# An attention and two-MLP kernel whose order is planned from a table of costs: the costs and the priorities are replaced

## The chip, the core and the metric

The kernel runs on one core of a Trainium2 chip. The metric is the time of one execution on the device, in microseconds (us). TensorE (PE in the rows) does the matmuls, VectorE (DVE) and ScalarE (ACT) the elementwise work, GpSimd (POOL) next to nothing here, and the queues of SyncE (SP) and ACT issue the transfers.

## What is computed

Attention over 2 batches of 8 heads, 768 positions of 64 values, in which a query sees only the keys of its own hash bucket (6 sign bits of a projection); then two MLPs on the 1536 tokens, the first with a softplus, the second with a hard swish.

```python
mask = q_bucket[:, :, :, None] == k_bucket[:, :, None, :]
scores = np.where(mask, scale * np.matmul(q, k.transpose(0, 1, 3, 2)), -1000000000.0)
attn = np.exp(scores - np.max(scores, axis=-1, keepdims=True))
attn = attn / (np.sum(attn, axis=-1, keepdims=True) + 1e-09)
x = np.matmul(attn, v)                     # then heads side by side: 1536 x 512
h = x @ w_in                               # 512 x 2048, float64 weights
x = (np.maximum(h, 0.0) + np.log1p(np.exp(-np.abs(h)))) @ w_out
h = x @ w2_in
out = (h * np.clip(h + 3.0, 0.0, 6.0) / 6.0) @ w2_out
```

## The kernel before

**Attention.** There are 16 heads, and each has six tiles of 128 queries. `prepare` (L296) loads a head, splits q and k into a high part (`qa`, `ka`, on ACT at L331 and L243) and a low part (`qb`, `kb`, on DVE at L338 and L248), computes the hash products `d` on PE (L373) and turns them into bits that are sent to spare rows of `qb` and `kb`. `attend` (L419) does per tile t: four score matmuls into `sc` (L431, L432), the row maximum on DVE (`nm`, L445), a bias and scale (`bs`, L452), the exponential on ACT (`e`, L460), six transposes on PE into `tp` (L471), and a copy out of PSUM to `et` (L243 on ACT, or L245 on DVE for tiles 0 and 3). When a head's six tiles are done, the products with v go to `av` (L487) in three pieces of four; then come a copy `xa`, three transposes `pt` (L509), the normalisation `xn` (L524), and for every second head six transposes `xt` (L551) that lay the result out as MLP input.

`sc` and `tp` share three PSUM buffers (`THREE`), so a new `sc` can be written only when the `tp` that was three buffers ahead of it has been copied out. All of `raw`, `qa`, `ka`, `qb`, `kb` have two buffers, so head h+2 takes the place of head h: `ka` of head h+2 can be written only when head h's last score has been computed.

**MLPs.** `hidden` (L646) multiplies tokens with `w_in` into `ph` (L656), `activation` (L671) works on ACT and DVE, `project` (L737) multiplies with `w_out` into `acc` (L749, L751). A product is made of three matmuls, with high and low parts. The weights are float64 in memory; `convert` (L577) makes two float32 parts of each of the 64 blocks, with two operations on ACT and five on DVE. Sixteen blocks (`lows`) are loaded on ACT's queue and converted while attention runs, the other 48 in the MLPs. The first `hidden` matmul is planned after the last score of head 15 (`gate["hidden"]`).

**What sets the order.** No order is written by hand. Every piece of work is an operation with a cost per engine, and `Schedule.run` (L105) plays them through: it takes the engine and time that end first, and among the operations that could start there the one with the lowest `prio`. A head's priorities are `h * TH` plus a number from the table `WHEN`. The engines then execute exactly the order that came out, each its own, one after the other. So the costs and priorities leave no trace in the program but the order, and on which of two engines a copy stands. A `lows` block may not be converted before its `early` time (L580), nor loaded before `early - 12`.

Of the kernel before, what the change touches and what calls it, by code (L numbers as in the profile page):

```python
# [15 lines left out]
AF = mybir.ActivationFunctionType  # L16
# [19 lines left out]
TH = 10.540  # L36
WHEN = dict(load_p=-19.19, load_k=-22.30, load_q=-10.44, load_v=-16.15, high_k=-3.85, high_q=-7.91, low_k=7.98, low_q=-13.35, copy_q=2.17, dots=-7.44, bits=-3.01, send=-4.68, scores=0.99, max=-17.09, exp=5.00, turn=1.96, even=3.05, values=19.12, back=24.61, rec=19.19, norm=8.42, x=22.28, x_high=27.35, x_low=11.84)
# [10 lines left out]
STEP = 6.328  # L48
PROJECT = 9.472
ACTIVATE = -20.197  # L50
FETCH = -64.944
AHEAD = 22.618


def f32(ap):
    return ap.bitcast(F32)

# [22 lines left out]
class Schedule:  # L80
# [8 lines left out]
    def add(self, cost, emit, reads=(), writes=(), prio=0.0, after=(), uses=(), dma=0.0, mode="r", early=0.0):  # L89
# [15 lines left out]
    def run(self):  # L105
# [3 lines left out]
        while ready:  # L109
# [48 lines left out]
    def times(self, op):  # L158

        return {  # L160
            e: max([op.early] + [d.done + (SAME[e] if d.engine == e else CROSS) for d in op.deps]) for e in op.cost
        }

    def free(self, b, tag, taken):
# [7 lines left out]
        return max([o.done + CROSS for o in ring[i].users], default=0.0)  # L172
# [14 lines left out]
def lsh_attention_two_mlps(  # L187
# [90 lines left out]
    for s0, e in ((0, "S"), (D, "A")):  # L278
        plan.add(
            {e: 0.625 if e == "S" else 0.06}, lambda e, s0=s0: engines[e].dma_start(out=p32.ap[s0 : s0 + D, :], in_=proj),  # L280
            writes=[p32], prio=WHEN["load_p"], dma=0.06,
        )
# [13 lines left out]
    def prepare(h):  # L296
# [7 lines left out]
        queue = dict(S=0.625, A=0.06)  # L304
        first = queue if h > 1 else dict(S=0.625)
        plan.add(
            first, lambda e: engines[e].dma_start(out=raw.ap[0:D, :], in_=kv[head][0:D, :S]),
            writes=[raw], prio=at + WHEN["load_k"], dma=0.55,
# [3 lines left out]
            writes=[raw], prio=at + WHEN["load_k"], dma=0.55,  # L312
        )
        if h:
# [3 lines left out]
                writes=[rawk], prio=at + WHEN["load_q"], dma=1.1,  # L318
            )
        plan.add(  # L320
            dict(S=0.625),
            lambda e: engines[e].dma_start(out=vx[h].ap, in_=kv[head][:, S:].rearrange("p (c d) -> p c d", d=D)),
            writes=[vx[h]], prio=at + WHEN["load_v"], dma=1.1,
        )

        wide, narrow = dict(A=0.74) if h else dict(A=0.74, D=0.48), dict(D=0.88)
# [16 lines left out]
        if h:  # L343
            plan.add(
                wide, lambda e: cast(e, ka[h].ap, rawk.ap),
                reads=[rawk], writes=[ka[h]], prio=at + WHEN["high_k"],
            )
        else:
            for s0, e in ((0, "D"), (D, "A")):
                plan.add(  # L350
                    {e: wide[e]}, lambda e, s0=s0: cast(e, ka[h].ap[s0 : s0 + D, :], raw.ap[0:D, :]),
# [3 lines left out]
            narrow, lambda e: minus(e, kb[h].ap[0:D, :], raw.ap[0:D, :], f32(ka[h].ap[0:D, :])),  # L355
            reads=[raw, ka[h]], writes=[kb[h]], prio=at + WHEN["low_k"],
        )
        if h:
            plan.add(
                queue, lambda e: engines[e].dma_start(out=f32(qb[h].ap[0:D, :]), in_=f32(qa[h].ap[D:P, :])),  # L360
                reads=[qa[h]], writes=[qb[h]], prio=at + WHEN["copy_q"], dma=0.55,
            )
        else:
            plan.add(
                dict(A=0.74), lambda e: cast(e, qb[h].ap[0:D, :], f32(qa[h].ap[D:P, :])),
# [12 lines left out]
        plan.add(dict(T=0.68), dot, mode="c", reads=[raw, hashes], writes=[dots], prio=at + WHEN["dots"])  # L378
        if h == 0:
            for u in range(2):  # L380
                for n, x in enumerate((qb, kb)):
                    rows = slice((2 * u + n) * ROWS, (2 * u + n + 1) * ROWS)
                    plan.add(
                        dict(D=0.5),
# [15 lines left out]
        for u in range(2):  # L400
            for n, x in enumerate((qb, kb)):
# [6 lines left out]
                    reads=[bits], writes=[x[h]], prio=at + WHEN["send"], dma=0.15,  # L408
# [5 lines left out]
    def attend(h):  # L414
# [19 lines left out]
        for t in range(NT):  # L434
# [3 lines left out]
            for u in range(2):  # L438
                last_scores = plan.add(
                    dict(T=0.356), lambda e, sc=sc, t=t, u=u: scores(sc, t, u),  # L440
# [3 lines left out]
                dict(D=0.88),  # L444
# [6 lines left out]
                dict(D=0.1),  # L451
# [6 lines left out]
            exp = plan.add(  # L458
                dict(A=1.08),
# [13 lines left out]
            plan.add(dict(T=0.5), turn, mode="t", reads=[ex, ident], writes=[tp], prio=step + WHEN["turn"])  # L473

            def even(e, tp=tp, t=t):
# [4 lines left out]
                dict(A=0.73) if t % 3 else dict(A=0.73, D=0.88), even, reads=[tp], writes=[et[t // n]], prio=step + WHEN["even"],  # L480
# [12 lines left out]
        for c in range(0, NT, 2):  # L493
            last = [
                plan.add(
                    dict(T=1.36), mode="c", emit=lambda e, c=c: [some(c), some(c + 1)],
# [5 lines left out]
            dict(A=0.44), lambda e: cast(e, xa.ap, av.ap[:, :HALF]),  # L502
# [8 lines left out]
        plan.add(dict(T=0.25), back, mode="t", reads=[xa, ident], writes=[pt], prio=at + WHEN["back"])  # L511
# [17 lines left out]
        plan.add(dict(D=0.5), norm, reads=[pt, rec], writes=[x], prio=at + WHEN["norm"])  # L529
        return last_scores, exp  # L530
# [11 lines left out]
    def to_features(hp_all, first, n):  # L542
# [6 lines left out]
        def turn(e):  # L549
# [3 lines left out]
        plan.add(dict(T=0.085 * n), turn, mode="t", reads=[xn[hp_all], ident], writes=[pt], prio=at + WHEN["x"])  # L553
        hi = plan.add(
            dict(A=0.053 + 0.107 * n), lambda e: cast(e, place(xh), pt.ap[:, : n * P]),
# [3 lines left out]
            dict(D=0.069 + 0.133 * n), lambda e: minus(e, place(xl), pt.ap[:, : n * P], f32(place(xh))),  # L559
# [17 lines left out]
    def convert(layer, j, i, prio, after=()):  # L577

        before = layer == 0 and (j, i) in lows
        early = (lows.index((j, i)) + 1) * B * H * TH / (len(lows) + 1) if before else 0.0  # L580
# [18 lines left out]
        queue = dict(A=0.06) if before else dict(S=0.625)  # L599
# [204 lines left out]
    for h in range(B * H):  # L804
        prepare(h)
        last_scores, exp = attend(h)
        if h == 0:
            first_exp = exp
# [68 lines left out]
```

## Time and profile before

| | us |
|---|---|
| median of 3 runs | 804.89 |
| lowest and highest | 803.55, 804.92 |
| the profiled execution's own time | 804.03 |
| its span in the trace | 802.2 |
| PE, DVE, ACT busy in it | 776.2, 533.9, 483.8 |

The span runs from the first instruction to the last; the execution's time holds 1.8 us around it. An instruction's listed time is from its own start to its end, and instructions of one engine overlap a little, so the pace of an engine is read from start to start. In the trace a matmul of full float32 (`av`, `d`) stands as two instructions.

### The profile page before, as it was taken

The page shows a single profiled execution, that of the slowest core. Times are in us where ns is not written, and L with a number is a line of the kernel's source. Part 1 is how long each engine was busy: PE and PEld are TensorE (multiplying, and loading weights), DVE is VectorE, ACT ScalarE, POOL GpSimd, SP SyncE. Part 2 cuts the span into 40 slices and gives each one's busy share as a digit, 9 for nine tenths or more (in the row PEclk, how much of TensorE's full clock was granted, in tenths as well). Part 3 has the DMA queues.
Part 4 walks back from the last instruction along what each step waited for, and adds up shares of the span by engine and source line. Part 5 has one row for each costly group of instructions (what it writes and reads, how often), then busy time and mean ns, then how long its engine had stood idle before and what let it go on. Part 6 is the DMA issues. An engine that isn't in the chain of part 4 may idle for free.

```text
span 802.2 us, 10347 instructions
## 1 busy us (share of the span) xinstructions
PE 776.2 (97%) x3808; PEld 598.8 (75%) x3808; DVE 533.9 (67%) x942; ACT 483.8 (60%) x817; POOL 9.3 (1%) x53
## 2 busy tenths in 40 slices
PE   6799999999999999999999999999999999999997
PEld 3566666666667788888888888878888888888886
DVE  6699899886765899965554789999972322232222
ACT  4688998888875877766556677765642322231222
POOL 1000000000000000000000000000000000000000
PEclk9999999999999999999999999999999999999999
DMA  6545445432310460000000355640000100010001
GB/s 177 164 139 144 125 150 151 120 113 77 90 31 11 160 259 2 0 1 1 0 1 1 92 196 192 203 149 9 1 0 1 54 0 1 1 52 1 1 0 53
DMA packets 26355, 58.61 MB, mean 73 GB/s; under 512 B 3585, under 2 KB 7553, under 8 KB 26305
## 3 DMA queue, kind: packets, MB, share of 16 engines
q1 hardware_dynamic: 22128, 49.56, 20.2%
q10 hardware_dynamic: 4176, 8.39, 3.4%
q8 instruction: 30, 0.49, 0.3%
q14 instruction: 21, 0.16, 0.1%
HBM read 48.89 MB, written 3.15 MB: 65 GB/s over the span
## 4 chain that ended last, share of the span: by engine, by line
PE 87%; ACT 7%; DVE 3%; DMA 2%; issue 1%; SPq 0%; ACTq 0%; DVEq 0%
PE ph L656 33%; PE acc L749 17%; PE acc L751 16%; PE av L487 7%; PE tp L471 6%; PE sc L431 4%; PE sc L432 3%; ACT e L460 3%; ACT et L243 2%; DMA raw<-in_moe_w_in_dram 1%; ACT qa L331 1%; DVE nm L445 1%; ACT ka L243 1%; PE pt L509 1%; DVE qa L338 0%
## 5 line engine op out<-in xcount | busy, mean ns | idle before, releaser
L656 PE MATMUL ph<-xh,w 128*128 128x512 f32 x768 | 239.0, 393 | 0.0
L656 PEld LDWEIGHTS ph<-xh,w 128*128 128x128 f32 x768 | 144.0, 188 | 31.7
L656 PE MATMUL ph<-xl,w 128*128 128x512 f32 x384 | 150.4, 392 | 0.0
L685 DVE SCALAR_TENSOR_TENSOR ml<-me,ph 128x512 f32<-128x512 f32 x48 | 33.0, 688 | 114.1 <-ACT me L680 113.9
L460 ACT ACTIVATE e<-sc,bs 128x768 f32<-128x768 f32 x96 | 94.8, 989 | 22.5 <-DVE bs L452 21.9
L445 DVE TENSOR_REDUCE nm<-sc 128x1 f32<-128x768 f32 x96 | 89.5, 951 | 25.7 <-PE sc L432 25.4
L680 ACT ACTIVATE me<-ph,three 128x512 f32<-128x512 f32 x48 | 33.0, 688 | 122.0 <-PE ph L656 118.9
L749 PE MATMUL acc<-gh,w 128*128 128x512 f32 x384 | 98.3, 394 | 0.0
L751 PE MATMUL acc<-w,gh 128*128 128x512 f32 x384 | 97.4, 392 | 0.0
L471 PEld LDWEIGHTS tp<-ident,e 128*128 128x128 f32 x576 | 63.6, 142 | 37.1 <-ACT e L460 22.4
L471 PE MATMUL tp<-ident,e 128*128 128x128 f32 x576 | 80.0, 280 | 7.2 <-ACT e L460 6.2
L749 PEld LDWEIGHTS acc<-gh,w 128*128 128x128 f32 x384 | 71.7, 188 | 17.4 <-ACT gh L243 0.8
L751 PEld LDWEIGHTS acc<-w,gh 128*128 128x128 f32 x384 | 72.2, 188 | 16.2
L656 PEld LDWEIGHTS ph<-xl,w 128*128 128x128 f32 x384 | 72.2, 188 | 15.9
L431 PE MATMUL sc<-ka,qa 128*128 128x384 f32 x192 | 73.3, 382 | 6.1 <-ACT et L243 5.4
L487 PE MATMUL av<-et,vx 128*64 128x384 f32 x384 | 71.4, 498 | 0.0
L243 ACT ACTIVATE et<-tp 128x768 f32<-128x768 f32 x78 | 62.5, 811 | 12.6 <-PE tp L471 11.9
L432 PE MATMUL sc<-kb,qb 96*128 96x384 f32 x192 | 66.5, 346 | 0.4 <-DVE kb L385 0.4
L716 DVE SCALAR_TENSOR_TENSOR me<-mu,me 128x512 f32<-128x512 f32 x48 | 33.1, 690 | 38.3 <-ACT mu L711 38.1
L749 PE MATMUL acc<-gl,w 128*128 128x512 f32 x192 | 53.4, 393 | 0.7 <-ACT xh L243 0.7
L243 ACT ACTIVATE gh<-ml 128x512 fp32r<-128x512 f32 x48 | 30.1, 628 | 38.3 <-DVE ml L728 38.3
L751 PE MATMUL acc<-w,gl 128*128 128x512 f32 x192 | 53.1, 391 | 0.0
(65 smaller groups left out, 957.0 us busy)
## 6 DMA issues: line engine op xcount, KB each, us to landing
raw<-in_moe_w_out_dram SPq DMA_DIRECT2D x30, 512.0 KB, 4.2
raw<-in_moe_w_in_dram SPq DMA_DIRECT2D x18, 512.0 KB, 4.7
raw<-in_moe_w_in_dram ACTq DMA_DIRECT2D x14, 512.0 KB, 4.1
rawk<-in_kv_dram SPq DMA_DIRECT2D x15, 384.0 KB, 3.5
raw<-in_kv_dram SPq DMA_DIRECT2D x16, 192.0 KB, 3.6
raw<-in_q_dram SPq DMA_DIRECT2D x16, 192.0 KB, 3.7
vx<-in_kv_dram SPq DMA_DIRECT2D x16, 192.0 KB, 2.6
out_dram<-y SPq DMA_DIRECT2D x12, 256.0 KB, 2.0
```

Source lines behind the costliest of these rows:

```text
L243: nc.scalar.activation(out, in_, AF.Copy)
L431: nc.tensor.matmul(o, qa[h].ap[:, qs], ka[h].ap[:, cs], start=True, stop=False)
L432: nc.tensor.matmul(o, qb[h].ap[0:KB, qs], kb[h].ap[0:KB, cs], start=False, stop=True)
L445: lambda e, sc=sc, t=t: nc.vector.reduce_max(nm.ap[:, t, 0:1], sc.ap[:, :, :HALF], axis=AX.XY, negate=True),
L460: lambda e, sc=sc, ex=ex, t=t: nc.scalar.activation(ex.ap.rearrange("p (u k) -> p u k", u=2), sc.ap[:, :, :HALF], AF.Exp, bias=bs.ap[:, t, ...
L471: nc.tensor.transpose(o, ex.ap[:, c * P : (c + 1) * P], ident.ap)
L487: nc.tensor.matmul(av.ap[u * D : (u + 1) * D, :HALF], vx[h].ap[:, c, :], et[u].ap[:, c, :], start=(c == 0), stop=(c == NT - 1),)
L656: nc.tensor.matmul(bank(), w[:, a, :], x[b].ap[:, kc, :], start=(kc + i == 0), stop=(kc == KC - 1 and i == 2))
L680: dict(A=0.478), lambda e: nc.scalar.activation(e1.ap, bank(), AF.Relu, bias=three.ap),
L716: lambda e: nc.vector.scalar_tensor_tensor(e1.ap, u.ap, -1.0, e1.ap, op0=ALU.add, op1=ALU.subtract),
L749: nc.tensor.matmul(o, w.ap[:, a, cs], b.ap, start=st, stop=sp)
L751: nc.tensor.matmul(o, b.ap[:, cs], w.ap[:, a, :], start=st, stop=sp)
```

## The change

The instructions and the data that each computes stay as they are; every cost that the planner uses, the table of priorities, the model of a transfer and the release times of the 16 early weight blocks are replaced. The core of the diff (the same kind of edit of a cost is made at every operation; each row of the table is a number):

```diff
-TH = 10.540
-WHEN = dict(load_p=-19.19, ..., scores=0.99, max=-17.09, exp=5.00, turn=1.96, even=3.05, values=19.12, ...)
-CROSS = 0.2
-SAME = dict(A=0.13, D=0.13, P=0.1, T=0.0, S=0.0, H=0.0)
-SWITCH = dict(rt=0.1, rc=0.15, tr=0.1, tc=0.25, cr=0.1, ct=0.05)
-STAY = 2.103
-ISSUE, LATENCY, DONE = 0.625, 0.65, 0.74
+TH = 16.41
+WHEN = dict(load_p=-69.22, ..., scores=-1.98, max=-149.65, exp=-149.76, turn=-8.77, even=-56.85, values=53.65, ...)
+CROSS = dict(TA=0.2, TD=0.2, TS=0.2, AT=0.16, AD=0.135, AS=0.12, AP=0.19, DA=0.16, DT=0.15, ...)
+SAME = dict(A=0.13, D=0.05, P=0.1, T=0.0, S=0.0, H=0.0)
+SWITCH = dict(rt=0.0, rc=0.138, tr=0.007, tc=0.145, cr=0.205, ct=0.156)
+STAY = 10.971
+ISSUE, SETUP, LANDED = 0.6, 1.3, 0.4
+START, EVERY = 33.82, 14.426
...
-                free["M"] = max(start + ISSUE + LATENCY, free["M"]) + op.dma
-                op.done = free["M"] + DONE
+                moved, least = op.dma
+                free["M"] = max(start + SETUP, free["M"]) + moved
+                op.done = max(start + least, free["M"] + LANDED)
...
-                dict(A=1.08),
+                dict(A=0.967),
-            plan.add(dict(T=0.5), turn, mode="t", ...
+            plan.add(dict(T=0.655), turn, mode="t", ...
-                dict(A=0.73) if t % 3 else dict(A=0.73, D=0.88), even, ...
+                dict(A=0.692) if t % 3 else dict(A=0.692, D=0.867), even, ...
-        early = (lows.index((j, i)) + 1) * B * H * TH / (len(lows) + 1) if before else 0.0
+        early = START + EVERY * lows.index((j, i)) if before else 0.0
...
-    convert_all(0, lows, [first_exp])
+    convert_all(0, lows)
```

`STAY` is what an operation of another kind (scores `r`, transposes `t`, full float32 `c`) must be ahead in priority for PE to leave the kind that it is in.

The first place is PE at the turn from head 5 to head 6 (`d8` the hash products of head 8, `tp5_3` to `tp5_5` the transposes of head 5's second three tiles, `sc6_0` the scores of head 6's first tile, whose pair of rows stands twice in the program). Before:

```order
L373 MATMUL d8_1158<-raw8_1086,hash_76 64x384 x2
L471 MATMUL tp5_3_1171<-ident_102,e5_3_1155 128x128 x6
L471 MATMUL tp5_4_1182<-ident_102,e5_4_1164 128x128 x6
L431 MATMUL sc6_0_1194<-ka6_1048,qa6_964 128x384
L432 MATMUL sc6_0_1194<-kb6_966,qb6_958 128x384
L471 MATMUL tp5_5_1207<-ident_102,e5_5_1192 128x128 x6
```

and now:

```order
L379 MATMUL d8_1116<-raw8_1047,hash_76 64x384 x2
L477 MATMUL tp5_3_1120<-ident_102,e5_3_1105 128x128 x6
L477 MATMUL tp5_4_1132<-ident_102,e5_4_1112 128x128 x6
L477 MATMUL tp5_5_1146<-ident_102,e5_5_1128 128x128 x6
L437 MATMUL sc6_0_1156<-ka6_917,qa6_996 128x384
L438 MATMUL sc6_0_1156<-kb6_924,qb6_915 128x384
```

The three transposes now stand together ahead of the next scores. In heads 2 to 15, but for a swap of neighbours in heads 11 and 12, PE now goes through one sequence: three tiles of scores, `pt` of two heads back, eight rows of `av` of the head before, three tiles of transposes, three tiles of scores, the last four rows of `av`, `d` of head h+3 (up to head 15's), three tiles of transposes; in odd heads two `xt` groups stand inside it. Before, scores, transposes and `av` were mixed in another way in nearly every head, with `av` mostly in three pieces and single transposes between score tiles.

The second place is ACT in the second half of head 6 (`e6_3` the exponential of tile 3, `ka8` and `qa8` the high parts of head 8, `xa5` the copy of head 5's `av`, `et6_1` the copies of head 6's transposes). Before:

```order
L460 ACTIVATE e6_3_1318,den6_1242<-sc6_3_1285,bs6_1225 128x768
L243 ACTIVATE xa5_1324<-av5_1245 128x384
L460 ACTIVATE e6_4_1343,den6_1242<-sc6_4_1302,bs6_1225 128x768
L331 ACTIVATE qa8_1353<-raw8_1086 64x768
L243 ACTIVATE ka8_1366<-rawk8_1059 128x768
L243 ACTIVATE et6_1_1345<-tp6_4_1357 128x6x128
L460 ACTIVATE e6_5_1389,den6_1242<-sc6_5_1321,bs6_1225 128x768
```

and now:

```order
L609 ACTIVATE bits0_1_1_1258<-raw0_1_1_1189 128x512
L249 ACTIVATE ka8_1264<-rawk8_962 128x768
L466 ACTIVATE e6_3_1274,den6_1199<-sc6_3_1240,bs6_1183 128x768
L466 ACTIVATE e6_4_1280,den6_1199<-sc6_4_1246,bs6_1183 128x768
L466 ACTIVATE e6_5_1297,den6_1199<-sc6_5_1251,bs6_1183 128x768
L249 ACTIVATE xa5_1311<-av5_1193 128x384
L600 DMA raw0_2_0_1324<-in_moe_w_in_dram 128x2x256
L249 ACTIVATE et6_1_1307<-tp6_4_1300 128x6x128
L249 ACTIVATE et6_1_1307<-tp6_5_1315 128x6x128
L337 ACTIVATE qa8_1343<-raw8_1047 64x768
L249 ACTIVATE w0_1_1_1349<-bits0_1_1_1258 128x512
```

The three exponentials now follow each other, with `ka` of the head after next just ahead of them and `qa` behind them. One weight block is loaded and converted per head from head 1 to head 15 and one in the MLPs; before, several were taken in some heads, and all sixteen were done by head 10.

## Rows read from the trace of the kernel before

**Rows 1.** Page: busy us (share of the span) xinstructions of each engine
```profile
PE 776.2 (97%) x3808; PEld 598.8 (75%) x3808; DVE 533.9 (67%) x942; ACT 483.8 (60%) x817; POOL 9.3 (1%) x53
```
**Rows 2.** Stretches: start:end, length, busy us (instructions) per engine, granted clock, DMA share, GB/s
```profile
25.00:248.00 223.00, 210.33 (x1308) 142.68 (x1309) 185.20 (x345) 188.16 (x325) 6.64 (x29) 1.00 0.43 118
45.00:171.00 126.00, 121.66 (x762) 82.91 (x761) 115.98 (x218) 111.93 (x196) 4.26 (x17) 1.00 0.50 140
171.00:248.00 77.00, 73.05 (x457) 49.87 (x456) 53.89 (x100) 61.27 (x106) 1.61 (x9) 1.00 0.24 63
300.00:350.00 50.00, 50.00 (x218) 40.56 (x217) 46.49 (x83) 35.65 (x63) 0.00 (x0) 1.00 0.00 1
```
**Rows 3.** Timeline of PE (start, us, operation): first score of heads 1 and 15, first MLP matmul
```profile
24.87 0.44 PE L431 MATMUL sc<-ka,qa 128*128 128x384 f32 x1 [0.26 <-DVE et L245]
...
248.25 0.42 PE L431 MATMUL sc<-ka,qa 128*128 128x384 f32 x1
...
260.23 0.71 PE L656 MATMUL ph<-xh,w 128*128 128x512 f32 x2
```
**Rows 4.** Timeline of PE, two waits inside attention
```profile
39.63 0.45 PE L431 MATMUL sc<-ka,qa 128*128 128x384 f32 x1 [2.08 <-ACT et L243]
...
236.05 0.87 PE L471 MATMUL tp<-ident,e 128*128 128x128 f32 x6 [1.05 <-ACT e L460]
```
**Rows 5.** Timeline of PE, second half of head 9 and first half of head 10
```profile
163.20 0.42 PE L431 MATMUL sc<-ka,qa 128*128 128x384 f32 x1
...
165.50 2.80 PE L487 MATMUL av<-et,vx 128*64 128x384 f32 x16
168.13 0.82 PE L373 MATMUL d<-raw,hash 128*64 128x384 f32 x4
168.88 2.19 PE L471 MATMUL tp<-ident,e 128*128 128x128 f32 x18
170.82 0.43 PE L431 MATMUL sc<-ka,qa 128*128 128x384 f32 x1
...
173.21 0.49 PE L509 MATMUL pt<-ident,xa 128*128 128x128 f32 x3
173.64 2.80 PE L487 MATMUL av<-et,vx 128*64 128x384 f32 x16
176.37 1.53 PE L471 MATMUL tp<-ident,e 128*128 128x128 f32 x12
```
**Rows 6.** Groups by line from 20 to 260 us, the layout transposes of PE
```profile
L551 PE MATMUL xt<-ident,xn 128*128 128x128 f32 x42 | 7.2, 285 | 0.7 <-DVE xn L524 0.7
```
**Rows 7.** Timeline of DVE, the first two row maxima of head 10
```profile
172.52 1.81 DVE L445 TENSOR_REDUCE nm<-sc 128x1 f32<-128x768 f32 x2
```
**Rows 8.** Timeline of ACT, second half of head 9 and first of head 10
```profile
166.30 0.84 ACT L243 ACTIVATE ka<-rawk 128x768 fp32r<-128x768 f32 x1
167.05 0.97 ACT L460 ACTIVATE e<-sc,bs 128x768 f32<-128x768 f32 x1
...
168.02 0.98 ACT L460 ACTIVATE e<-sc,bs 128x768 f32<-128x768 f32 x1
...
171.52 0.82 ACT L243 ACTIVATE et<-tp 128x768 f32<-128x768 f32 x1
...
174.52 0.99 ACT L460 ACTIVATE e<-sc,bs 128x768 f32<-128x768 f32 x1 [1.12 <-DVE bs L452]
```
**Rows 9.** Timeline of ACT, a weight block that ACT waits for
```profile
38.21 0.66 ACT L603 ACTIVATE bits<-raw 128x512 f32<-128x512 f32 x1 [3.48 <-DMA raw<-in_moe_w_in_dram]
```
**Rows 10.** Transfers issued on ACT's queue: count, KB each, median us to landing
```profile
raw<-in_moe_w_in_dram ACTq DMA_DIRECT2D x14, 512.0 KB, 4.1
...
raw<-in_moe_w_out_dram ACTq DMA_DIRECT2D x2, 512.0 KB, 10.0
```
**Rows 11.** Timeline of PE, two neighbouring score matmuls of head 0
```profile
12.30 0.52 PE L432 MATMUL sc<-kb,qb 96*128 96x384 f32 x1
12.62 0.52 PE L431 MATMUL sc<-ka,qa 128*128 128x384 f32 x1
```

More of the change, by code (lines that the diff above doesn't have):

```diff
@@ L87, in __init__, with add @@
         self.ops, self.rings = [], {}
-    def add(self, cost, emit, reads=(), writes=(), prio=0.0, after=(), uses=(), dma=0.0, mode="r", early=0.0):
+    def add(self, cost, emit, reads=(), writes=(), prio=0.0, after=(), uses=(), dma=None, mode="r", early=0.0):
         deps = list(after)
@@ L160, in times @@
         return {
-            e: max([op.early] + [d.done + (SAME[e] if d.engine == e else CROSS) for d in op.deps]) for e in op.cost
+            e: max([op.early] + [d.done + between(d.engine, e) for d in op.deps]) for e in op.cost
         }
@@ L171, in free @@
             return math.inf
-        return max([o.done + CROSS for o in ring[i].users], default=0.0)
+        return max([o.done + 0.2 for o in ring[i].users], default=0.0)
     def slots(self, op):
@@ L303, in prepare @@
         vx[h] = buffer("tail", [P, NT, D], F32, "vx", 2, f"vx{h}")
-        queue = dict(S=0.625, A=0.06)
-        first = queue if h > 1 else dict(S=0.625)
+        queue = dict(S=0.6, A=0.06)
+        first = queue if h > 1 else dict(S=0.6)
         plan.add(
             first, lambda e: engines[e].dma_start(out=raw.ap[0:D, :], in_=kv[head][0:D, :S]),
-            writes=[raw], prio=at + WHEN["load_k"], dma=0.55,
+            writes=[raw], prio=at + WHEN["load_k"], dma=(0.85, 3.2),
         )
@@ L376, in dot @@
                 )
-        plan.add(dict(T=0.68), dot, mode="c", reads=[raw, hashes], writes=[dots], prio=at + WHEN["dots"])
+        plan.add(dict(T=0.646), dot, mode="c", reads=[raw, hashes], writes=[dots], prio=at + WHEN["dots"])
         if h == 0:
@@ L457, in attend @@
             )
-            exp = plan.add(
-                dict(A=1.08),
+            plan.add(
+                dict(A=0.967),
                 lambda e, sc=sc, ex=ex, t=t: nc.scalar.activation(
@@ L471, in turn @@
                     nc.tensor.transpose(o, ex.ap[:, c * P : (c + 1) * P], ident.ap)
-            plan.add(dict(T=0.5), turn, mode="t", reads=[ex, ident], writes=[tp], prio=step + WHEN["turn"])
+            plan.add(dict(T=0.655), turn, mode="t", reads=[ex, ident], writes=[tp], prio=step + WHEN["turn"])
             def even(e, tp=tp, t=t):
@@ L495, in attend @@
                 plan.add(
-                    dict(T=1.36), mode="c", emit=lambda e, c=c: [some(c), some(c + 1)],
+                    dict(T=1.29), mode="c", emit=lambda e, c=c: [some(c), some(c + 1)],
                     reads=[*et, vx[h]], writes=[av], prio=at + c * TH / NT + WHEN["values"], after=last,
@@ L509, in back @@
                 nc.tensor.transpose(pt.ap[:, i * P : (i + 1) * P], xa.ap[:, i * P : (i + 1) * P], ident.ap)
-        plan.add(dict(T=0.25), back, mode="t", reads=[xa, ident], writes=[pt], prio=at + WHEN["back"])
+        plan.add(dict(T=0.33), back, mode="t", reads=[xa, ident], writes=[pt], prio=at + WHEN["back"])
         plan.add(
@@ L527, in norm @@
             )
-        plan.add(dict(D=0.5), norm, reads=[pt, rec], writes=[x], prio=at + WHEN["norm"])
-        return last_scores, exp
+        plan.add(dict(D=0.464), norm, reads=[pt, rec], writes=[x], prio=at + WHEN["norm"])
+        return last_scores
     xh, xl = {}, {}
@@ L551, in turn @@
                 nc.tensor.transpose(pt.ap[:, i * P : (i + 1) * P], xn[hp_all].ap[:, first + i, :], ident.ap)
-        plan.add(dict(T=0.085 * n), turn, mode="t", reads=[xn[hp_all], ident], writes=[pt], prio=at + WHEN["x"])
+        plan.add(dict(T=0.11 * n), turn, mode="t", reads=[xn[hp_all], ident], writes=[pt], prio=at + WHEN["x"])
         hi = plan.add(
-            dict(A=0.053 + 0.107 * n), lambda e: cast(e, place(xh), pt.ap[:, : n * P]),
+            dict(A=0.052 + 0.106 * n), lambda e: cast(e, place(xh), pt.ap[:, : n * P]),
             reads=[pt], writes=[xh[0, g]], prio=at + WHEN["x_high"],
@@ L597, in convert @@
         low, high = lambda: words()[:, :, 0], lambda: words()[:, :, 1]
-        queue = dict(A=0.06) if before else dict(S=0.625)
-        plan.add(queue, load, writes=[raw], prio=prio[0], after=after, dma=1.456, early=early - 12)
+        queue = dict(A=0.06) if before else dict(S=0.6)
+        plan.add(queue, load, writes=[raw], prio=prio[0], after=after, dma=(2.2, 3.2), early=early - 12)
         plan.add(
-            dict(A=0.52), lambda e: nc.scalar.activation(f32(b.ap), f32(high()), AF.Abs),
+            dict(A=0.565), lambda e: nc.scalar.activation(f32(b.ap), f32(high()), AF.Abs),
             reads=[raw], writes=[b], prio=prio[1], early=early,
@@ L663, in hidden @@
                 plan.add(
-                    dict(T=0.687), lambda e, kc=kc: some(kc),
+                    dict(T=0.686), lambda e, kc=kc: some(kc),
                     reads=[W[layer, j, kc // 2], *x], writes=[ph], prio=prio, after=last,
@@ L727, in activation @@
         plan.add(
-            dict(D=0.63), lambda e: engines[e].tensor_tensor(l.ap, l.ap, e1.ap, op=ALU.add),
+            dict(D=0.602), lambda e: engines[e].tensor_tensor(l.ap, l.ap, e1.ap, op=ALU.add),
             reads=[l, e1], writes=[l], prio=prio,
```

89 lines of the change are left out of this document (45 added, 44 removed).

## The prediction

> **What bounds the kernel now.** I read the page first: PE is listed busy for 97% of the span [rows 1]. That does not say that PE works at its pace all the time, because a listed matmul goes on while the next has begun. So I counted instructions in stretches. In the MLPs PE runs 218 matmuls in 50 us and has no idle time [rows 2]; the change leaves these matmuls alone, and they already follow each other without a gap. From the first MLP matmul at 260.23 us [rows 3] to the end of the span it is 802.2 - 260.2 = 542 us, and I expect this part to stay. All that can be won lies before it.
>
> Inside attention the useful measure is the time of a head. Head 1's first score starts at 24.87 us and head 15's at 248.25 [rows 3]: 223.4 us for 14 heads, 15.96 us each. What holds a head up? The obvious suspect is DVE, listed busy for 116 of 126 us from 45 to 171 us, where it converts most of the early weight blocks. But from 171 to 248 us, with no block left for the last part of it, DVE is listed for only 54 of 77 us, and PE goes no faster: 762 matmuls in 126 us are 6.05 per us, 457 in 77 us are 5.94 [rows 2]. So the release of the blocks alone buys little. What the two stretches share is short waits for results that are not there yet: PE's transposes wait 1.05 us for an exponential, its scores 2.08 us for a copy out of the buffer that they need [rows 4]. The order puts too little other work between a result's start and its use. That is what the change replaces.
>
> **The new order, step by step.** No operation is added or removed, so the sum is the time of a head in the new sequence, times 14, plus the start.
>
> *PE's own work in a head.* The sequence that every head now has stands once in the old trace, from head 9's second half into head 10 [rows 5]. From start to start there: three score tiles 165.50 - 163.20 = 2.30 us; sixteen `av` instructions and `d` 168.88 - 165.50 = 3.38, of which `d` is 0.75, so that four rows of `av`, half of them, are 1.32; three tiles of transposes 170.82 - 168.88 = 1.94; `pt` 173.64 - 173.21 = 0.43; sixteen more `av` instructions, which are eight rows of the order, 176.37 - 173.64 = 2.73. A head takes scores twice (4.60), transposes twice (3.88), `pt` 0.43, `av` 2.73 + 1.32, `d` 0.75: 13.71 us. The `xt` are three per head on average; listed they take 7.2 us for 42 [rows 6], 0.17 each or 0.51 a head, while at the transposes' pace (1.94 / 18) they take 0.32. I take 0.4. PE alone would need 14.1 us a head.
>
> *Does the chain of maximum, exponential and copy fit under it?* First half: the two maxima of head 10 start at 172.52 [rows 7] and the first exponential at 174.52 [rows 8], 2.0 us later; the others follow every 0.97 us (168.02 - 167.05) [rows 8]. Scores start at 0, the first tile is done after 0.77, and with a hand-over of 0.2 the first maximum starts at about 0.95; so the exponentials end at 3.9, 4.9 and 5.8 us. PE is at scores, `pt` and `av` until 2.30 + 0.43 + 2.73 = 5.46, and the three transposes start at 5.5, 6.1 and 6.8: covered. The copies then run on ACT from 6.3 to 8.4, each 0.7 us (listed at 0.82 [rows 8], with the overlap that all listed times have), and each frees its buffer some 0.2 us before PE comes to the score tile that takes it (7.4, 8.2, 8.9): covered, with little to spare.
>
> Second half, counted from its first score: `ka` of head h+2 stands ahead of the exponentials and must wait for the last score of head h at 2.3, since it overwrites that head's `ka`. It takes 167.05 - 166.30 = 0.75 [rows 8], so the exponentials end at 4.0, 5.0 and 6.0 us. PE has only four rows of `av` and `d` as cover: 2.30 + 1.32 + 0.75 = 4.4. The first transposes start at once, the second want 5.0 plus some 0.2 us of hand-over against 5.05, the third 6.2 against 5.85. That is a wait of about 0.45 us a head, which no other work covers. Hence **14.1 + 0.45 = 14.55 us a head**.
>
> *The start.* Head 0 keeps its loads and its first three score tiles. But all six of its transposes now stand ahead of head 1's first score, which before passed two of them: 2 x 1.94 / 3 = 1.3 us later, less some of head 0's short waits, the last of which is the 0.26 us in [rows 3]. I put head 1's first score at 25.6 us; 24.6 and 27 are the bounds: a second wait like the 1.05 us in [rows 4] gone, or one more of that kind.
>
> *The weights.* One block a head now goes through ACT and DVE instead of several in some heads, and no longer are four loads issued at once, which had ACT stand for 3.48 us until the first landed [rows 9]. About one and a half blocks move into the first MLP group, some 2.5 us of DVE each. There DVE is listed for 46.5 of 50 us and PE still has no idle [rows 2]; listed times overlap (two maxima are listed at 1.81 us together, 0.95 alone) [rows 7], so there is room. I take nothing for it; the bound is 3.7 us.
>
> *ACT.* From 25 to 248 us ACT is listed for 188 us [rows 2], 13.4 a head, with overlaps in it. Under 14.55 it fits, at 92%, and is the next to bind.
>
> *The sum.* Head 15 starts at 25.6 + 14 x 14.55 = 229.3 us instead of 248.25 [rows 3], 18.95 us earlier. From there to the first MLP matmul the new order has the same work but one transposed tile more and one `pt` less, about 0.3 us, which are then missing or due behind it: no difference. The profiled execution took 804.03 us, so 785.1; the median stands 0.86 above it, so **786 us** against 804.89.
>
> **A rule that speaks against the change.** After the eighteen transposes at 168.88 us the twelve score matmuls from 170.82 to 173.21 start 0.20 us apart on average, and the granted clock is 1.00 [rows 2, 5], the upper of the two levels (2.4 GHz). The Trainium skill, "TensorE: Matmul & The Clock Gate", section on the PE-mode transpose, says that transposes do not count as work for the clock as matmuls do; by that, three tiles of transposes in a row could bring the lower level, and the trace here does not agree.
>
> **The rivals.**
>
> - *PE at its own pace.* If the waits of the second half vanish, because ACT gets ahead, a head takes 14.1 us: 582.2 + 14 x 14.1 = 780 us (582.2 is 804.89 - 248.25 + 25.6). For it: the old trace runs this piece without a listed wait [rows 5]. Against it: there eight rows of `av` covered the second half, and now four.
> - *Hand-overs a little longer in both halves.* The copies of the first half were covered by 0.2 us only. If they miss by 0.2 to 0.3 us each and the second half waits 0.6, a head takes 15.2 us: 795 us. For it: ACT at over 90%, and an order that is good only if each duration is what the planner thinks.
> - *The change does not do what it says.* The order differs, but other waits of the same size take the place of those removed: 15.96 us a head, 805 us, a little over or under no change. Against it: the piece in [rows 5] ran in this order with no listed wait of PE.
> - *Slower: ACT stands waiting for the weight block.* The block's first operation stands ahead of `ka` and the three exponentials, so if the block has not landed, all of attention waits. Its load is issued one half and a bit earlier on ACT's own queue: behind it come two copies, `qa`, a weight part, three exponentials and three copies, about 8.2 us. It decides from a landing over 8.2 us. For it: two of the sixteen blocks took 10.0 us [rows 10], and ACT did wait 3.48 us once [rows 9]. Against it: those were issued together; the other fourteen took 4.1 [rows 10]. At 10.0 us each of 14 heads loses 1.8 us: 786 + 25 = 811 us.
> - *Slower: the lower clock behind the transposes.* In head 0, before PE has been busy for long, neighbouring score matmuls start 0.32 us apart [rows 11] instead of 0.19. If the twelve score matmuls behind each of 30 groups of transposes ran so, each would lose 0.13 us: 47 us, 833 us. The rows of head 10 speak against it.
>
> **How the numbers follow.** A measurement of this kernel can tell about 0.2%, 1.6 us, from no change. The forecast (14.4 to 14.8 us a head) has 0.60 and covers 784 to 790 us. PE at its own pace has 0.15, the longer hand-overs 0.14, equal waits 0.05, the late weight block 0.05, the clock 0.01. The range goes from 777 (780, less what a better start and ACT's lost 3.48 us could add) to 796 (the longer hand-overs, or the forecast with 3.7 us given back in the MLPs and a late start). It leaves out equal waits, the two slower rivals and some of the edges, a little under 2 in 10. Faster by over 0.2%: 0.60 + 0.15 + 0.14 = 0.89. Equal waits give 0.03 to no change and 0.02 to slower; with the late block and the clock, slower has 0.08.
>
> **What would show it.** Head 15's first score at 227 to 232 us; 14.4 to 14.8 us from head to head, nearly constant; PE's second-half transposes waiting some 0.3 us for ACT's exponentials, and no score waiting for a copy by more than that; about 6.5 matmuls per us in attention (94 in a head) where 6.05 and 5.94 stood; from the first MLP matmul to the end 541 to 546 us. The prediction is wrong if scores wait for `et` in most heads, if ACT waits for a DMA in more than two heads, or if the MLP part grows by over 4 us.

## The result and the profile after

| | before | after |
|---|---|---|
| median (4 runs each) | 804.9 us | 787.3 us (785.56 to 787.43) |
| ratio, 95% interval | | 0.9777 [0.9757, 0.9797] |
| profiled execution / its span | 804.03 / 802.2 us | 787.35 / 785.6 us |
| head 1's / head 15's first score | 24.87 / 248.25 | 27.50 / 230.44 |
| first MLP matmul, from there to the end | 260.23, 541.97 | 242.87, 542.73 |

The forecast was 786 us, with 777 to 796 as its range. PE's timeline after, in the manner of [rows 3, 4] (line numbers are 6 higher now): the first transposes of head 0, the first scores of heads 1, 7, 8, 9 and 15, the hash products in head 7, the first MLP matmul.

```profile
17.12 3.71 PE L477 MATMUL tp<-ident,e 128*128 128x128 f32 x18 [2.24 <-ACT e L466]
...
27.50 0.42 PE L437 MATMUL sc<-ka,qa 128*128 128x384 f32 x1
...
114.02 0.42 PE L437 MATMUL sc<-ka,qa 128*128 128x384 f32 x1
...
126.50 0.87 PE L379 MATMUL d<-raw,hash 128*64 128x384 f32 x4 [0.58 <-PE av L493]
...
129.23 0.42 PE L437 MATMUL sc<-ka,qa 128*128 128x384 f32 x1
...
143.23 0.42 PE L437 MATMUL sc<-ka,qa 128*128 128x384 f32 x1
...
230.44 0.42 PE L437 MATMUL sc<-ka,qa 128*128 128x384 f32 x1
...
242.87 0.70 PE L662 MATMUL ph<-xh,w 128*128 128x512 f32 x2
```

From head 1 to head 15 a head takes (230.44 - 27.50) / 14 = 14.50 us, but from head 3 to head 10 by turns: 15.21 us from 114.02 to 129.23, then 14.00 (heads 11 to 14 take 14.78, 14.31, 14.60 and 14.31). Stretches after, as in [rows 2]:

```profile
17.10:18.50 1.40, 1.38 (x9) 1.12 (x10) 1.40 (x4) 1.40 (x3) 0.00 (x0) 0.72 0.86 279
18.50:20.50 2.00, 2.00 (x12) 2.00 (x11) 0.61 (x1) 1.24 (x3) 0.00 (x0) 0.50 0.97 206
...
45.00:171.00 126.00, 123.29 (x815) 89.52 (x811) 106.68 (x203) 117.49 (x204) 4.19 (x17) 1.00 0.44 127
171.00:228.00 57.00, 56.15 (x364) 40.25 (x363) 51.03 (x97) 50.01 (x89) 1.68 (x7) 1.00 0.36 105
300.00:350.00 50.00, 49.96 (x218) 40.37 (x217) 43.08 (x75) 35.34 (x63) 0.00 (x0) 1.00 0.00 0
```

PE does 815 / 126 = 6.47 matmuls per us where it did 6.05, DVE has come down from 115.98 to 106.68 us in the same stretch, ACT gone up. The first two rows are dear: behind 2.24 us of idle PE the granted clock falls to the lower of its levels (0.50 is 1.2 GHz), in the middle of head 0. PE's waits inside attention, of before (20 to 262 us) the two largest kinds, of after (20 to 245 us) all that are listed: us in total, times, longest. A wait that falls inside a listed group of matmuls is not in them and is read from start to start.

```profile
PE tp L471 <- ACT e L460: 6.0, 8, 1.1
PE sc L431 <- ACT et L243: 5.4, 8, 2.1
```
```profile
PE d L379 <- PE av L493: 2.3, 4, 0.6
PE tp L477 <- ACT e L466: 1.5, 3, 1.0
```

No wait of scores for copies is listed any more. New is the wait of `d`. It needs the PSUM bank of the second `xt` group, which DVE's `xl` frees, and `xl` stands behind a row maximum. DVE in head 7:

```profile
125.11 0.95 DVE L451 TENSOR_REDUCE nm<-sc 128x1 f32<-128x768 f32 x1
125.98 0.41 DVE L254 TENSOR_TENSOR xl<-xt,xh 128x256 fp32r<-128x256 f32 x1
```

`xl` ends at 126.39 and `d` starts at 126.50, though the profile names `av` as what released it. Only odd heads have `xt` groups, from head 3 on.

### The profile page after: what moved, and what is told of

Its sections match the earlier page's. It is cut to its first block, busy times and chain, and to the rows that moved or that the text cites. A ratio compares the mean times of both kernels' runs of the same rounds, so it can differ in the third digit from the quotient of the medians.

```text
span 785.6 us, 10356 instructions
## 1 busy us (share of the span) xinstructions
PE 764.9 (97%) x3808; PEld 599.1 (76%) x3808; DVE 529.0 (67%) x938; ACT 485.0 (62%) x821; POOL 9.5 (1%) x53
## 4 chain that ended last, share of the span: by engine, by line
PE 90%; ACT 4%; DVE 3%; issue 2%; DMA 1%; SPq 0%; ACTq 0%; DVEq 0%
PE ph L662 34%; PE acc L755 17%; PE acc L757 17%; PE tp L477 7%; PE av L493 6%; PE sc L437 4%; PE sc L438 3%; ACT e L466 2%; DVE nm L451 2%; PE xt L557 1%; ACT ka L249 1%; PE pt L515 1%; PE d L379 1%; DMA raw<-in_q_dram 1%; ACT et L249 0%
## 5 line engine op out<-in xcount | busy, mean ns | idle before, releaser
L477 PE MATMUL tp<-ident,e 128*128 128x128 f32 x576 | 76.6, 281 | 4.9 <-ACT e L466 3.8
L437 PE MATMUL sc<-ka,qa 128*128 128x384 f32 x192 | 69.1, 360 | 0.1
L493 PE MATMUL av<-et,vx 128*64 128x384 f32 x384 | 68.8, 494 | 0.0
```

The source lines that it names most:

```text
L437: nc.tensor.matmul(o, qa[h].ap[:, qs], ka[h].ap[:, cs], start=True, stop=False)
L477: nc.tensor.transpose(o, ex.ap[:, c * P : (c + 1) * P], ident.ap)
L493: nc.tensor.matmul(av.ap[u * D : (u + 1) * D, :HALF], vx[h].ap[:, c, :], et[u].ap[:, c, :], start=(c == 0), stop=(c == NT - 1),)
```

## The experiments

Twelve kernels ran. `plan.hold(b, a)` makes the planner place b after a; it adds no wait on the chip, and nothing computed changes. "h 1-6" and "h 6-15" are us per head from the first score of head 1 to that of 6, and from 6 to 15; "MLP" is the first MLP matmul and the rest of the span behind it. The ratio is to runs of the kernel before that were taken beside each kernel (medians 803.6 to 804.9). The order of the MLPs is left to the planner in all of them, so what a kernel gains or loses in the heads is read at head 15's first score.

| kernel | median | ratio to before | head 1 at | h 1-6 | h 6-15 | head 15 at | MLP |
|---|---|---|---|---|---|---|---|
| before | 804.9 | | 24.87 | 16.55 | 15.62 | 248.25 | 260.2 + 542.0 |
| after | 787.3 | 0.978 [0.976, 0.980] | 27.50 | 14.51 | 14.49 | 230.44 | 242.9 + 542.7 |
| 1 costs | 813.1 | 1.011 [1.009, 1.013] | 26.55 | 16.89 | 15.08 | 246.70 | 261.9 + 548.3 |
| 2 priorities | 813.0 | 1.011 [1.009, 1.013] | 24.27 | 15.99 | 16.02 | 248.43 | 264.2 + 546.2 |
| 3 release | 803.5 | 0.999 [0.998, 1.000] | 24.27 | 16.22 | 15.38 | 243.74 | 259.2 + 541.6 |
| 4 all but release | 797.2 | 0.991 [0.990, 0.993] | 26.98 | 15.90 | 14.82 | 239.88 | 254.6 + 541.3 |
| 5 PE's order alone | 808.4 | 1.006 [1.004, 1.009] | 30.52 | 15.68 | 15.67 | 249.95 | 261.7 + 544.8 |
| 10 PE's order, release | 819.8 | 1.019 [1.017, 1.021] | 28.43 | 16.31 | 15.86 | 252.75 | 268.6 + 548.0 |
| 11 three orders, release | 793.3 | 0.986 [0.984, 0.988] | 25.11 | 14.83 | 14.44 | 229.19 | 244.8 + 546.9 |
| 6 `xt` in the next head | 789.2 | 0.982 [0.980, 0.983] | 27.18 | 14.47 | 14.53 | 230.32 | 244.9 + 543.2 |
| 7 maximum first | 787.1 | 0.979 [0.977, 0.980] | 27.20 | 14.44 | 14.48 | 229.75 | 244.3 + 541.9 |
| 8 `ka` late | 792.0 | 0.985 [0.983, 0.986] | 26.30 | 14.78 | 14.72 | 232.71 | 245.3 + 544.1 |
| 9 three orders, new numbers | 794.3 | 0.987 [0.985, 0.989] | 24.20 | 15.33 | 14.72 | 233.30 | 245.5 + 547.3 |
| 12 maximum first, `d` later | 789.5 | 0.982 [0.981, 0.983] | 26.66 | 14.82 | 14.51 | 231.33 | 245.9 + 542.3 |

### One part of the change at a time (1 to 4)

Kernel 1 takes the changed kernel and puts back the old `TH`, `WHEN`, `STAY`, `STEP` to `AHEAD` and the old release; kernel 2 gives the kernel before those new numbers alone; kernel 3 is:

```diff
-        early = (lows.index((j, i)) + 1) * B * H * TH / (len(lows) + 1) if before else 0.0
+        early = 33.82 + 14.426 * lows.index((j, i)) if before else 0.0
...
-    convert_all(0, lows, [first_exp])
+    convert_all(0, lows)
```

and kernel 4 undoes just that in the changed kernel.

> The changed kernel with the old priorities and the old release of weight blocks; only the durations, hand-overs, mode switches and transfer times of the planner are new. TensorE's order: from head 6 on the projection's three groups stand together again, heads 1 to 5 are mixed. Theory 1 (true costs make the order in which every wait is covered, priorities and release only help to keep it): heads 6 to 14 at about 14.5 us each, heads 1 to 5 at 15.5 to 16, so 5 to 8 us over the changed kernel, 791 to 796 us. Theory 2 (the priorities make it): no gain over the kernel before, 802 to 806. Theory 3 (the even release of weight blocks makes it): the same, 802 to 806.

> The kernel before with the new priorities alone; costs, hand-overs and release stay old. TensorE's order is mixed in nearly all heads, single groups of transposes between scores and values. Theory 1: 799 to 808 us, within 0.7% of the kernel before. Theory 2: 787 to 792. Theory 3: 802 to 806.

> The kernel before with weight blocks released from 33.82 us on at 14.426 us each in place of multiples of 10.54; nothing else. TensorE's order stays mixed, the copies are spread over all heads. Theory 1: 800 to 806 us. Theory 2: 802 to 806. Theory 3 (VectorE relieved in heads 4 to 11, so that PSUM banks come free sooner): 787 to 795.

> The changed kernel with the old release of weight blocks alone (one per 10.54 us from the start); costs and priorities new. TensorE's order is the changed kernel's in heads 6 to 11 and mixed in 1 to 5 and 12 to 14. Theory 1: 14.5 us in the six regular heads, 15.3 to 16 in the others, 792 to 798 us. Theory 2: 787 to 790, as the changed kernel. Theory 3: 800 to 806, the whole gain gone, and VectorE's busy share in the heads with more blocks back at over 90%.

New costs alone or new priorities alone make the kernel slower, the release alone does nothing, costs and priorities together gain some 6 us, and the release then gives 10 more. But the loss of kernels 1 and 2 does not lie in the heads: their head 15 starts 1.55 us sooner and 0.18 later than in the kernel before (248.25), and 9.6 and 8.0 us are lost behind it, at the turn to the MLPs, where PE waits for the last transposed results. PE of kernel 1:

```profile
274.70 1.22 PE L662 MATMUL ph<-xh,w 128*128 128x512 f32 x2 [2.06 <-DVE xl L254]
```

The release alone is nothing only in the sum: head 15 starts 4.5 us sooner, and 3.2 of it are lost behind. Of the heads the four kernels say that no part alone brings the 14.50 us: costs 15.72, priorities 16.01, release 15.68, costs and priorities 15.21, before 15.96.

Theory 1 met kernels 3 and 4 and missed kernel 1 by 17 us and kernel 2 by 5; theories 2 and 3 fall. What the release does beside the rest is seen on DVE; from 45 to 100 us, of kernel 4 and of after:

```profile
45.00:100.00 55.00, 49.92 (x325) 35.51 (x326) 51.84 (x97) 45.80 (x83) 1.68 (x6) 1.00 0.51 142
```
```profile
45.00:100.00 55.00, 53.63 (x358) 38.69 (x354) 46.89 (x90) 51.28 (x90) 2.04 (x8) 1.00 0.42 121
```

DVE is listed for 94% where it is listed for 85% after, and PE does 325 matmuls instead of 358. In heads 1 to 5 of kernels 1 and 4 TensorE's order is broken, and what broke it is dear. `xt` stands in the first half there, so `av` waits for the bank that `xl` holds; in kernel 1 the granted clock then falls:

```profile
66.49 0.87 PE L493 MATMUL av<-et,vx 128*64 128x384 f32 x4 [2.17 <-DVE xl L254]
```
```profile
68.00:70.00 2.00, 2.00 (x11) 1.86 (x10) 1.93 (x6) 0.98 (x3) 0.00 (x0) 0.50 0.73 215
```

### The order on TensorE alone, and the orders of three engines (5, 10, 11)

A chain of holds fixes TensorE's order of all heads to that of the changed kernel, under the old numbers; it ends with head 15's transposes:

```diff
+    row = []
+    for h in range(B * H):
+        N = lambda *k: [named[k]] if k in named else []
+        row += [named["sc", h, t, u] for t in range(3) for u in range(2)] + N("pt", h - 2)
+        row += N("av", h - 1, 0) + N("av", h - 1, 1)
...
+    for a, b in zip(row, row[1:]):
+        plan.hold(b, a)
```

> The kernel before, with its old costs, priorities and release, but TensorE's order of all 16 heads fixed by hand to that of the changed kernel (three scores, eight and then four products with the values, three transposes). The other engines' orders and the transfers are the old planner's. Theory 1 (TensorE's order is the gain, whatever makes it): 786 to 792 us, 14.4 to 14.9 us per head. Theory 4 (the regular order needs the other engines' orders and the even release as well, since costs alone, with half of the heads regular, took 813 us): 797 to 806 us, with TensorE waiting in the regular order for exponentials or for a bank that VectorE holds.

> The kernel before, old costs and old priorities, TensorE's order fixed to that of the changed kernel, and the even release of weight blocks. Theory 5 (what the fixed order lacked was only the relief of VectorE, 98% busy in heads 2 to 5 of that run): 786 to 792 us. Theory 6 (the orders of ScalarE and VectorE, where the third exponential stands behind copies and roundings, make the transposes wait): 795 to 804 us, transposes waiting for exponentials by over 10 us in all.

TensorE's order is not the gain by itself, and relieving DVE does not mend that: 808.4 and 819.8 us. Theories 1 and 5 (786 to 792) fall. Theories 4 and 6 have the right kind of wait, transposes that wait for exponentials, 17.1 us of it in kernel 5 and 19.4 in kernel 10 (20 to 262 us), but both put the level too low (797 to 806, 795 to 804): neither foresaw a loss against the kernel before. Part of that loss is outside the steady heads. In kernel 5 a head takes 15.67 us, a little under before, while head 1 starts 5.65 us later; kernel 10 loses 9.9 us behind head 15. Kernel 10 in head 5, DVE first and then ACT:

```profile
104.35 0.42 DVE L253 TENSOR_TENSOR xl<-xt,xh 128x256 fp32r<-128x256 f32 x1 [1.21 <-ACT xh L248]
104.70 0.95 DVE L452 TENSOR_REDUCE nm<-sc 128x1 f32<-128x768 f32 x1
105.67 0.95 DVE L345 SCALAR_TENSOR_TENSOR qa<-raw,qa 64x768 fp32r<-64x768 f32 x1
106.66 0.16 DVE L459 SCALAR_TENSOR_TENSOR bs<-nm 128x2 f32<-128x2 f32 x1
```
```profile
103.95 0.38 ACT L248 ACTIVATE xh<-xt 128x256 fp32r<-128x256 f32 x1
104.35 0.84 ACT L338 ACTIVATE qa<-raw 64x768 fp32r<-64x768 f32 x1
105.21 0.84 ACT L248 ACTIVATE ka<-rawk 128x768 fp32r<-128x768 f32 x1
105.96 0.66 ACT L611 ACTIVATE bits<-raw 128x512 f32<-128x512 f32 x1
106.94 0.99 ACT L467 ACTIVATE e<-sc,bs 128x768 f32<-128x768 f32 x1 [0.32 <-DVE bs L459]
```

DVE stands 1.21 us before `xl`, since ACT comes to `xh` only behind two exponentials; the third maximum follows, then a `qa`, then its scale. So the third exponential comes 4 us after the second began, at 102.98, and this head takes 18.72 us (91.26 to 109.98), which also hold a wait of 1.97 us before the second `xt` group, at 102.62, and the low clock behind it (0.50 from 104.3 to 107.6). Kernel 11 orders the other two engines as well: the scale directly behind its maximum, three exponentials in a row, other work of ACT behind them. It also moves the second `xt` group and orders head 0 as kernels 6 and 12 do.

```diff
+    for h in range(2, B * H):
+        plan.hold(named["ka", h], named["exp", h - 2, 5])
+    for h in range(2, B * H):
+        plan.hold(named["qa", h], named["exp", h - 2, 5])
+    for h in range(B * H):
+        for t in (0, 3):
+            plan.hold(named["et", h, t], named["exp", h, t + 2])
+        if h:
+            plan.hold(named["xa", h - 1], named["exp", h, 5])
...
```

> The kernel before, old costs and old priorities, with all three engines' orders fixed as in e9_all_orders and the even release. Theory 6 (the planner's numbers count only through the orders that come out of them): within 3 us of e9_all_orders, 779 to 787 us. Rival (what is left to the planner, its loads, roundings and copies between the fixed operations, still needs the true durations): 790 to 800 us.

> The changed kernel with the orders of three engines fixed: TensorE as now but with the second feature transposes in the next even head and the fourth head's hash products after the second head's first scores; each row maximum with its scale directly behind it on VectorE; three exponentials in a row on ScalarE, with the copies of the values and of the transposes and the roundings of later heads behind them; head 0's VectorE as in the run before. Theory (the second half's transposes wait for an exponential whose scale stands behind the next maximum; with it directly behind, the exponentials start some 0.8 us sooner and the waits of 0.4 to 0.6 us that the last runs left go): 14.2 to 14.35 us per head, head 1's first score at 24.3 to 25.5 us, 779 to 783 us. Rival (ScalarE, busy for 94% of an even head, is the bound): 14.5 us per head and more, 785 to 790 us.

Kernel 11 comes to 793.3 us, 26.5 less than kernel 10 with the same numbers and the same release, and 23.6 of that lie before head 15. PE's waits for exponentials, of kernel 10 and of kernel 11 (20 to 262 us):

```profile
PE tp L478 <- ACT e L467: 19.4, 20, 1.9
```
```profile
PE tp L473 <- ACT e L462: 2.0, 6, 1.0
```

A head takes 14.58 us under the old numbers, against 14.50 in the changed kernel, and head 15 starts 1.25 us sooner than there. That is the best evidence that the numbers count through the orders. The total is within 3 us of kernel 9, as theory 6 said, but this is partly luck: kernel 9's heads take longer, 14.94 us, and behind head 15 it is the quicker one (against the changed kernel it loses 4.4 us there, kernel 11 7.4). The level was missed by 6 us and lies in the range of the rival (790 to 800), and where it was lost the rival has a point: the turn to the MLPs is left to the planner. There, in kernel 11, PE waits for the last layout transposes and runs at the low clock:

```profile
255.12 1.11 PE L554 MATMUL xt<-ident,xn 128*128 128x128 f32 x4 [1.66 <-DVE xl L253]
```
```profile
255.00:262.00 7.00, 5.58 (x15) 4.30 (x16) 6.94 (x16) 3.12 (x6) 0.00 (x0) 0.51 0.63 226
```

For kernel 9 theory and rival (779 to 790) were both too low. Kernel 9 removes most of the second half's waits for exponentials and lets head 1 start at 24.20, and some heads take 13.8 to 14.2 us, but the work put behind the exponentials now includes the copies that free PSUM, and scores wait for them. The worst of these waits is followed by the low clock:

```profile
54.88 0.44 PE L444 MATMUL sc<-ka,qa 128*128 128x384 f32 x1 [1.94 <-ACT et L254]
```
```profile
57.00:59.00 2.00, 2.00 (x8) 1.69 (x7) 1.70 (x4) 1.54 (x3) 0.00 (x0) 0.50 0.73 201
```

### The waits that the changed kernel has left (6, 7, 8, 12)

Kernel 6 holds the second `xt` group until the next even head's normalisation:

```diff
+    for n in range(B * H // 2 - 1):
+        plan.hold(named["xt", n, 4 if n < H // 2 else 2], named["norm", 2 * n + 2])
```

> The changed kernel, with the second group of feature transposes held until the normalisation of the next even head, so that it moves out of the odd head. Theory (the 0.58 us that the hash products of odd heads wait are for the PSUM bank of that group, held until VectorE's subtraction): odd heads 15.2 to 14.2 or 14.4, even heads 14.0 to 14.4 or 14.6, together 3 to 4 us less, 783 to 785 us. Rival (the odd heads' time is the exponentials' chain, and the bank's wait only covers it): the sum of two heads stays at 29.2 us, 786 to 788 us.

The wait of `d` is gone, which shows that the bank was its cause, and nothing is gained: heads take 14.49 and 14.86 by turns (99.51, 114.00, 128.86), 29.35 for two where it was 29.21. In head 7 the eighteen transposes behind `d` now take 2.58 us (126.28 to 128.86) instead of 1.93: they meet the exponentials. So the rival holds for the heads, and the bank's wait was cover for the same chain: head 15 starts at 230.32, as in the changed kernel (230.44). The 1.9 us by which the kernel is slower are lost behind head 15. The other three kernels of this section lose 1.3 to 1.7 us there as well.

Kernel 8 (`plan.hold(named["ka", h], named["exp", h - 2, 5])` alone):

> The changed kernel with the rounding of the keys of the head after next on ScalarE held until the last exponential of the head. Theory of the prediction (the transposes of the second half wait because that operation stands ahead of the exponentials): the wait of 0.36 us in the 7 even heads goes, 784.5 to 786 us. Rival (the same exponential waits as long for its scale on VectorE, which stands behind the second row maximum): at most 0.1 us per even head, 787 us, unchanged.

Neither number came: it is 5 us slower, and it does not tell the two causes apart, because the planner filled the gap with `qa`. ACT in head 6 of kernel 8:

```profile
109.88 0.84 ACT L344 ACTIVATE qa<-raw 64x768 fp32r<-64x768 f32 x1 [0.35 <-PE sc L444]
110.75 0.99 ACT L473 ACTIVATE e<-sc,bs 128x768 f32<-128x768 f32 x1
```

Kernel 7 lets head 0's row maxima go ahead of head 1's hash bits on DVE, with PE's order fixed to the changed kernel's own; kernel 12 in addition puts the fourth head's `d` behind head 1's first scores:

```diff
+    plan.hold(named["bits", 1], named["max", 0, 2])
+    plan.hold(named["low_q", 1], named["max", 0, 2])
```

> The changed kernel with TensorE's order fixed to its own, and the second head's hash bits and low part of the queries on VectorE held until the third row maximum of head 0. Theory (head 0 lost its time to an idle TensorE of 2.24 us before the first transposes and to the granted clock of 0.84 in 16 to 27 us that followed): first exponential at 14.3 in place of 15.9 us, idle time 0.6 us, granted clock 1.00, head 1's first score at 24.3 to 25.5 in place of 27.5, 784 to 786 us. Rival (what is held back comes late and head 1 waits for it): head 1's first score at 26.5 to 27.5, 787 us.

> The run e7_first_maximum_first with one more change: the hash products of the fourth head (the ones that waited 1.84 us for the load of its data) stand behind the first three scores of the second head instead of ahead of the second transposes of head 0. Theory (that wait and the low clock behind it hid the gain of the earlier row maximum): no idle time over 1.2 us on TensorE and a granted clock of 1.00 up to 30 us, head 1's first score at 24.2 to 25.2 in place of 27.2, all later heads as much sooner, 783 to 785.5 us. Rival (the later heads take it back through loads that come late): 786 to 788 us.

In kernel 7 the first exponential moves from 15.90 to 14.82 (14.3 was expected), and PE does not stand before the first transposes. But the operation that was held back reads the buffer into which the fourth head's data is loaded, so that load and `d` come late, and the clock falls there instead. In kernel 12 that wait is gone and the next one is as long. PE in kernel 7 and a stretch of it, then the same of kernel 12:

```profile
22.85 1.55 PE L386 MATMUL d<-raw,hash 128*64 128x384 f32 x4 [1.84 <-DMA raw<-in_q_dram]
```
```profile
24.00:27.00 3.00, 3.00 (x18) 2.67 (x17) 1.73 (x3) 1.77 (x4) 0.24 (x1) 0.62 0.82 260
```
```profile
23.47 3.53 PE L484 MATMUL tp<-ident,e 128*128 128x128 f32 x18 [1.88 <-ACT e L473]
```
```profile
25.00:27.00 2.00, 1.92 (x10) 1.62 (x9) 1.27 (x3) 1.95 (x4) 0.24 (x1) 0.53 0.77 220
```

Each time the rival's kind of answer came, kernel 12 a little above its numbers, and no version beat the changed kernel: kernel 7 is the same within its interval.

## Why the prediction came out, and where its steps failed

- **The time of a head** (14.55 forecast) measured 14.50, and "nearly constant" was wrong: 14.0 and 15.2. I had spread `xt` evenly at 0.4 us a head. It falls on odd heads alone, with the wait of `d` behind it, which I did not see. So the mean is right partly by luck: even heads take 14.0 us, the 13.71 of the sum and the second half's wait; odd heads take 1.5 us more than the 13.71, for six `xt` and a wait that the sum does not have.
- **The second-half wait** (0.45) is 0.36 in even heads: the transposes take 111.72 to 114.02, 2.30 us, instead of 1.94 [rows 5]. In odd heads the wait of `d` covers it; heads 13 and 14 have no `d` left as cover, and their transposes take 2.69 and 2.58 us. Its stated cause, `ka` ahead of the exponentials, does not hold by itself. The first exponential in head 6 starts when `ka` ends, but its scale, which stands behind the second maximum, is ready only then as well (ACT, then DVE):

```profile
109.57 0.84 ACT L249 ACTIVATE ka<-rawk 128x768 fp32r<-128x768 f32 x1 [0.51 <-PE sc L437]
110.32 0.99 ACT L466 ACTIVATE e<-sc,bs 128x768 f32<-128x768 f32 x1
```
```profile
110.07 0.28 DVE L458 SCALAR_TENSOR_TENSOR bs<-nm 128x2 f32<-128x2 f32 x2
```

In heads 1 to 10 the exponential starts 0.09 to 0.10 us behind the end of its scale. That is the same distance as in odd heads of kernel 6, where `ka` is done and the profile lists the exponential as waiting for the scale. ACT of kernel 6 in head 7:

```profile
125.14 0.99 ACT L473 ACTIVATE e<-sc,bs 128x768 f32<-128x768 f32 x1 [0.18 <-DVE bs L465]
```

So `ka` and the scale come at the same time, and moving `ka` alone could gain nothing.

- **The start** is the term that was mis-sized: 25.6 us forecast, bounds 24.6 to 27, measured 27.50. I priced the two transposed tiles more, and not the low clock. PE of before and of after:

```profile
9.45 0.69 PE L431 MATMUL sc<-ka,qa 128*128 128x384 f32 x1
...
16.38 2.33 PE L471 MATMUL tp<-ident,e 128*128 128x128 f32 x12 [0.15 <-ACT e L460]
```
```profile
10.20 0.69 PE L437 MATMUL sc<-ka,qa 128*128 128x384 f32 x1
...
13.40 0.34 PE L438 MATMUL sc<-kb,qb 96*128 96x384 f32 x1
13.58 0.34 PE L437 MATMUL sc<-ka,qa 128*128 128x384 f32 x1
```

The first transposes come 6.93 us behind the first score before and 6.92 after, so the 2.24 us of idle are no loss in themselves. Before, PE filled that time because its first scores ran 0.32 us apart [rows 11]; now they run 0.18 apart, PE is done early and stands. Why they run faster is not shown. The clock that falls behind the idle time is the loss: the eighteen transposes took 3.36 us (17.12 to 20.48) instead of 1.94, 1.42 more. A further 0.75 us lie before the first score (10.20 against 9.45); kernel 6, with the same order in head 0, has it at 9.65, so that most of this is not the change. Head 15 started at 230.44, not 229.3: the start's 1.9 us, less 0.7 that the heads gave back.
- **From head 15 on**: 12.43 us to the first MLP matmul where I had 11.98, and 542.7 where I had 542. The misses sum to 1.1 + 0.45 + 0.76 = 2.3 us over the 785.1 forecast for the profiled execution, which took 787.35.
- **"The release of the blocks alone buys little"** is right to the word (0.999), and misleads: in the new order it is worth 797.2 - 787.3 = 9.9 us, more than half of the gain. I argued from the old order, where PE went no faster with DVE less loaded [rows 2].
- **"The order puts too little other work between a result's start and its use"** is right as a diagnosis, and I looked for it on PE alone. With PE's order and nothing else a head takes 15.67 us and the kernel is slower (kernel 5). The piece of the old trace that I took as template [rows 5, 7, 8] had the matching orders on DVE and ACT as well, and I costed it without saying that it needs them.
- **The rivals.** Of the three that give another time of a head, 14.1, 15.2 and 15.96 us, none fits the 14.50 measured. Weight blocks land in 4.8 us on ACT's queue (14 transfers), and ACT waits for none. Behind groups of eighteen transposes the granted clock stays at 1.00 from 45 to 171 us, so the Trainium skill's rule ("TensorE: Matmul & The Clock Gate", section on the PE-mode transpose) is again not what this trace shows; where the clock fell, in head 0, PE had stood idle first.

## What to carry to other kernels

A planner's numbers act only through the orders that come out of them, and orders of several engines pay together: a part tried alone can be slower (813 us) or neutral (803.5) and still be most of the gain in company. Read such trials by stage: two of them were slower only where the heads give over to the MLPs. When one piece of a trace runs well, copy the orders of all engines that feed it. Moving the operation that a wait seems to blame often only uncovers the next late result, so look first at what else that result stands behind.

## What was not expected of the hardware

An idle TensorE costs more than the idle time. Behind 2.24 us here, 2.17 us in kernel 1, 1.84 in kernel 7, 1.88 in kernel 12 and 1.94 in kernel 9 the granted clock fell, down to 0.50 where a stretch was short enough to show it. It is no rule by length: the 2.08 us in [rows 4] and 2.23 us in kernel 4 were followed by 1.00; of before, and of kernel 4 behind its wait:

```profile
39.60:45.00 5.40, 4.63 (x28) 2.58 (x29) 4.95 (x10) 5.35 (x9) 0.11 (x1) 1.00 0.31 84
```
```profile
66.90:75.00 8.10, 7.72 (x50) 4.42 (x50) 7.97 (x17) 7.16 (x14) 0.11 (x1) 1.00 0.35 96
```

What else decides stays open. The price can be read from the changed kernel's four runs: three at a mean clock of 0.998 took 787.25 to 787.43 us, one at 1.000 took 785.56, 1.7 to 1.9 us less. The kernel before shows the same: of its 13 runs beside kernels 1 to 4 the six at 0.995 took 804.9 to 805.4 us, the seven at 0.997 to 0.999 803.0 to 803.6.
